# k and q of batch 0 loaded in two halves each, transposed in four groups, with the a1 copies on two engines around v's permute

## The chip, the cores and the metric

One core of a Trainium2 chip runs the kernel. The metric is the device time of one execution in microseconds (us). Most executions of one kernel agree within 0.3%. The profile's span is about 1.7 us shorter than the time (248.2 for 249.9). A run is called slow when it is over 1.5% above the fastest of its kernel.

## The reference, cut to what matters

```python
def sm_attn(qq, kk, vv):                   # q, k, v: 8 batches, 8 heads, 576 rows, 64
    s = scale * np.matmul(qq, kk.transpose(0, 1, 3, 2))
    a = softmax(s)                         # cut: max, exp, sum
    return np.matmul(a, vv)
p_packed = sm_attn(p, k, v)                # p: 32 rows per head
out = sm_attn(q, p_packed, p_packed)
# heads are joined to x (4608 x 512), then:
h = x @ w_in                               # 512 x 2048
return (h * np.cos(h)) @ w_out             # 2048 x 512
```

## The kernel before

The kernel works batch by batch. k and q have to be transposed by the matmul engine (PE), copied out of PSUM, where PE puts its results, by VectorE (DVE) or ScalarE (ACT), and multiplied. All large loads are issued from GpSimd (POOL) and convert float32 to bfloat16 on the way. In the listing, `s1` is the first softmax and a1 its exponentials, `pp` is a1 times v, `ppw` multiplies pp by a block of w_in (the result is PPW), and `s2` is the second softmax, with q. The opening, cut:

```python
def load(n, b):
    bf[n, b] = bf_pool.tile([TP, H, C * D], BF16, ...)       # 96 x 8 x 384
    G.dma_start(out=bf[n, b], in_=srcs[n][b].rearrange("h (p c) d -> p h (c d)", c=C))

def pe_T(n, b, engs, groups=(0, 1, 2), own=False):
    for i in groups:                                          # 3 groups of 8 transposes
        ...
        copy(engs[i], t[:, 8*i:8*i+8]..., ps[:, 0:8*TP])

nc.sync.dma_start(out=p_raw[:, 0:2, :], in_=p_rows[:, 0:2, :])
load("k", 0)
load("v", 0)
make_identity(nc, ident)
load("q", 0)
load("k", 1)
for n in range(3):
    load_w_in(n)
...                                       # constants
warm(7)                                   # matmuls on zeros, meant to keep PE's clock up
dup_p(0, 2, V); pack_p(0, 1)
warm(9)
pe_T("k", 0, (V, ACT, V))
ACT.dma_start(out=p_raw[:, 2:4, :], in_=p_rows[:, 2:4, :])
s1(0)                                     # first softmax: scores and exp
permute_v(0, V)
load("v", 1); load_w_in(3)
warm(3)
a1_pe(0)                                  # transposes of a1, copies by V
warm(2)
recips(0)
pp(0)                                     # a1 times v
pe_T("q", 0, (V, ACT, V))
load("q", 1)
for n in range(4):
    load_w_out(n)
G.dma_start(out=p_raw[:, 4:, :], in_=p_rows[:, 4:, :])
...
for fc in range(NFC):                     # h of batch 0, 16 steps
    rest = h_mm(0, fc)
    if fc in (11, 12, 13):
        pe_T("q", 1, (V, ACT, V), (fc - 11,), own=True)
    ...                                   # ppw at 1, 5, 8; pp(1) at 10; set_filler(0) at 13
    if fc >= 14:
        fill(2)                           # fill(n): n output matmuls (they need w_out)
...
fill(14)
slot(1, ...)                              # h of batch 1
```

The softmax here doesn't subtract the row's maximum and nothing guards it: scores larger than these inputs give would overflow.

Of the kernel before, what the change touches and what calls it, by code (L numbers as in the profile page):

```python
# [15 lines left out]
def kernel(  # L16
# [11 lines left out]
    B, H, S, D = q.shape  # L28
# [4 lines left out]
    C = 6  # L33
    TP = S // C
# [20 lines left out]
    V, ACT, G = nc.vector, nc.scalar, nc.gpsimd  # L55
# [13 lines left out]
    srcs = {"k": k, "q": q, "v": v}  # L69
    bf, vp, xT, a1T, sums1, r1, rs1 = {}, {}, {}, {}, {}, {}, {}  # L70
    a2u, lns, a2n, PPW = {}, {}, {}, {}

    def copy(eng, out, in_):
        if eng is ACT:
            ACT.copy(out=out, in_=in_)  # L75
        else:
            eng.tensor_copy(out=out, in_=in_)  # L77

    def psa(dt=FP32):
        return A.tile([128, 2, 512 if dt == FP32 else 1024], dt, name="psA", tag="A")  # L80

    def load(n, b):
        bf[n, b] = bf_pool.tile([TP, H, C * D], BF16, name=n + "bf", tag=n + "bf", bufs=2 if n == "k" else 1)
        G.dma_start(out=bf[n, b], in_=srcs[n][b].rearrange("h (p c) d -> p h (c d)", c=C))

    def permute_v(b, eng=G):
        vp[b] = vp_pool.tile([TP, C, H * D], BF16, name="vp", tag="vp")
        copy(eng, vp[b].rearrange("p c (h d) -> p c h d", h=H),
             bf["v", b].rearrange("p h (c d) -> p c h d", c=C))
# [2 lines left out]
        t = xT[n, b] = att_pool.tile([128, H * 3, TP], BF16, name=n + "T", tag=n + "T", bufs=2 if n == "k" else 1)  # L92
        nc.sync.dma_start_transpose(out=t, in_=bf[n, b].rearrange("p h x -> p (h x)"))

    def pe_T(n, b, engs=(V, V, V), groups=(0, 1, 2), own=False):
        if 0 in groups:
            xT[n, b] = att_pool.tile([128, H * 3, TP], BF16, name=n + "T", tag=n + "T", bufs=2 if n == "k" else 1)
        t = xT[n, b]
        flat = bf[n, b].rearrange("p h x -> p (h x)")
        for i in groups:  # L100
            ps = bank(BF16) if own else psa(BF16)[:, 0, :]
            for j in range(8):
                o = 8 * i + j
                nc.tensor.transpose(ps[:, j * TP:(j + 1) * TP], flat[:, o * 128:(o + 1) * 128],  # L104
                                    ident[0:TP, 0:TP])
            copy(engs[i], t[:, 8 * i:8 * i + 8].rearrange("p a x -> p (a x)"),
                 ps[:, 0:8 * TP])

    def bank(dt=FP32):
        return O.tile([128, 512 if dt == FP32 else 1024], dt, name="ot", tag="ot")  # L110

    def pack_p(b0, b1, flat=None):
        ng = 2 * (b1 - b0)
        if flat is None:
            flat = psa(BF16).rearrange("p a x -> p (a x)")
        for g in range(ng):
            nc.tensor.transpose(flat[:, g * 128:(g + 1) * 128],
                                p_bf[:, 2 * b0 + g].rearrange("p t d -> p (t d)"), ident)
        V.tensor_copy(out=P2[:, b0:b1].rearrange("p b h n -> p (b h n)"), in_=flat[:, 0:ng * 128])
# [14 lines left out]
    def s1(b, later=False):  # L134
        ps = scores(P2[:, b], xT["k", b])
        sm = sums1[b] = small.tile([128, 2], FP32, name="sums1")

        def exps():
            for y in range(2):
                ACT.activation(  # L140
                    out=a1[b % 2][:, y, :, 0:TP].rearrange("p (e m) x -> p e m x", e=2),
                    in_=ps[y][:, :, 0:HS].rearrange("p e (m x) -> p e m x", m=3),
                    func=AF.Exp, scale=scale, accum_out=sm[:, y:y + 1])
        if later:
            return exps
        exps()

    def recips(b):
        r1[b] = small.tile([128, 2], FP32, name="r1")
        rs1[b] = small.tile([128, 2], FP32, name="rs1")  # L150
        V.reciprocal(r1[b], sums1[b])
        V.tensor_scalar(out=rs1[b], in0=r1[b], scalar1=scale, scalar2=None, op0=ALU.mult)
# [3 lines left out]
        nc.sync.dma_start_transpose(out=t.rearrange("p a c x -> p (a c) x"),  # L156
                                    in_=a1[b % 2].rearrange("p a c x -> p (a c x)"))

    def a1_pe(b, ys=(0, 1), own=False):
        if 0 in ys:  # L160
            a1T[b] = att_pool.tile([128, 2, C, 128], BF16, name="a1T", tag="a1T")
        t = a1T[b]
        for y in ys:
            ps = bank(BF16) if own else psa(BF16)[:, 0, :]
            for c in range(C):
                nc.tensor.transpose(ps[0:TP, c * 128:(c + 1) * 128], a1[b % 2][:, y, c, 0:TP], ident)
            copy(V, t[0:TP, y].rearrange("p c x -> p (c x)"), ps[0:TP, 0:C * 128])

    def a1_one(b):
        t = a1T[b] = att_pool.tile([128, 2, C, 128], BF16, name="a1T", tag="a1T")  # L170
# [7 lines left out]
    def pp(b, own=False, engs=(V, ACT)):  # L178
        ps = bank() if own else psa()[:, 0, :]
        for hp in range(4):  # L180
            for j in range(C):
                c = 2 * (j % 3) + j // 3
                nc.tensor.matmul(ps[:, hp * 64:(hp + 1) * 64], vp[b][:, c, hp * 128:(hp + 1) * 128],  # L183
                                 a1T[b][0:TP, :, j, 32 * hp:32 * hp + 32], start=(j == 0), stop=(j == C - 1))
        pv = ps[:, 0:256].rearrange("p (a y x) -> p a y x", a=4, y=2)
        t = ppT[b % 2].rearrange("p (a y) x -> p a y x", y=2)
        for y in range(2):
            r = slice(64 * y, 64 * y + 64)
            copy(engs[0], t[r, :, y, :], pv[r, :, y, :])
        for y in range(2):  # L190
            r = slice(64 * y, 64 * y + 64)
            z = slice(64 - 64 * y, 128 - 64 * y)
            copy(engs[1], t[z, :, y, :], pv[r, :, y, :])
# [150 lines left out]
    def warm(n):  # L344
        wps = bank()
        for _ in range(n):
            nc.tensor.matmul(wps, wz[:, 0:128], wz, start=True, stop=True)  # L347

    nc.sync.dma_start(out=p_raw[:, 0:2, :], in_=p_rows[:, 0:2, :])
    load("k", 0)  # L350
    load("v", 0)
    make_identity(nc, ident)
    load("q", 0)
    load("k", 1)
    for n in range(3):
        load_w_in(n)
# [9 lines left out]
    warm(7)  # L366
    dup_p(0, 2, V)
    pack_p(0, 1)
    warm(9)
    pe_T("k", 0, (V, ACT, V))  # L370
    ACT.dma_start(out=p_raw[:, 2:4, :], in_=p_rows[:, 2:4, :])
    s1(0)
    permute_v(0, V)
    load("v", 1)
    load_w_in(3)
    warm(3)
    a1_pe(0)
    warm(2)
    recips(0)
    pp(0)  # L380
    pe_T("q", 0, (V, ACT, V))
    load("q", 1)
    for n in range(4):
        load_w_out(n)
# [5 lines left out]
    sums2(0, 0)  # L390
    sums2(0, 1)
    pe_T("k", 1, (V, V, V))
    warm(2)
    s1_mm = s1(1, later=True)
# [75 lines left out]
    s1(2)  # L470
    fill(5)
    a1_pe(2, (0,))
    fill(2)
    a1_pe(2, (1,))
    recips(2)
    fill(4)
# [94 lines left out]
```

## Time and profile before

| | before |
|---|---|
| median of the time, 6 runs | 249.91 us (249.81 to 250.28) |
| span of the profiled run | 248.2 us |
| PE, DVE, ACT busy | 234.5, 168.0, 166.9 us |
| first exponential of the first softmax (L140) | 9.78 us |
| first exponential of the second softmax (L225) | 16.05 us |
| k, q of batch 1 landed | 18.10, 33.43 us |
| last block of w_out landed | 43.70 us |

A landing is the moment at which the last of the 16 DMA engines has reported its share of a load; such times are from the trace's completion records.

### The profile page before, as it was taken

What the parts mean: (1) busy time and instruction counts of PE and PEld (TensorE: products, weight loads), DVE (VectorE), ACT (ScalarE), POOL (GpSimd) and SP (SyncE); (2) the same over time, 40 slices, a digit from 0 to 9 for tenths busy, and PEclk for the clock granted to TensorE, in tenths of its full rate; (3) what the DMA queues carried; (4) which work ended last, traced back from release to release, by engine and by line L of the source; (5) the groups of instructions that cost most, each with busy time, mean ns of one, the idle gap of its engine ahead of it and who ended that gap; (6) DMA issues with size and microseconds to landing.
All of it is one profiled execution on the core that took longest, in us unless ns stands there. A gap on an engine that the chain in (4) does not pass through costs nothing.

```text
span 248.2 us, 5035 instructions
## 1 busy us (share of the span) xinstructions
PE 234.5 (94%) x2003; PEld 131.6 (53%) x2037; DVE 168.0 (68%) x254; ACT 166.9 (67%) x278; POOL 54.8 (22%) x68
## 2 busy tenths in 40 slices
PE   8878799999999899999999999999999999999993
PEld 3454374566544654475546554565456554665452
DVE  2549987789568967678857766678766774876110
ACT  2368799746566787888877777888787684873000
POOL 8333533240400044022313105030500000000000
PEclk9999999999999999999999999999999999999999
DMA  6999999999899999999989995989491113201133
GB/s 91 203 203 206 205 206 229 200 241 153 162 206 219 167 158 220 206 193 173 190 162 192 174 194 68 177 164 209 103 156 33 45 42 82 47 26 58 46 83 85
DMA packets 63175, 37.09 MB, mean 149 GB/s; under 512 B 35792, under 2 KB 58576, under 8 KB 63152
## 3 DMA queue, kind: packets, MB, share of 16 engines
q0 software_dynamic: 23152, 18.75, 49.5%
q1 hardware_dynamic: 39568, 17.83, 34.3%
q8 instruction: 16, 0.26, 0.4%
q10 hardware_dynamic: 432, 0.20, 0.4%
q14 instruction: 7, 0.06, 0.1%
HBM read 37.22 MB, written 9.44 MB: 188 GB/s over the span
## 4 chain that ended last, share of the span: by engine, by line
PE 75%; DMA 9%; DVE 7%; ACT 5%; issue 2%; SPq 0%; DVEq 0%; ACTq 0%
PE ot L309 42%; PE psA L256 19%; DMA qbf<-in_q_dram 7%; DVE gT L263 4%; PE psA L207 3%; PE ot L347 3%; PE psA L183 2%; ACT cosT L260 2%; DMA out_dram<-osb 2%; PE psA L129 2%; PE ot L295 1%; PE psA L233 1%; DVE PPW L77 1%; ACT ppT L75 1%; PE psA L104 1%
## 5 line engine op out<-in xcount | busy, mean ns | idle before, releaser
L309 PE MATMUL ot<-w_out_bf,gT 128*128 128x512 bf16 x482 | 127.4, 379 | 2.1 <-issue 1.3
L263 DVE TENSOR_TENSOR gT<-psA,cosT 128x576 bf16<-128x576 f32 x128 | 93.6, 755 | 26.5 <-ACT cosT L260 25.9
L260 ACT ACTIVATE cosT<-psA 128x576 bf16<-128x576 f32 x128 | 82.5, 652 | 28.0 <-PE psA L256 23.2
L256 PE MATMUL psA<-a2n,PPW 128*128 128x288 bf16 x512 | 83.8, 286 | 1.9 <-DVE PPW L77 0.4
L309 PEld LDWEIGHTS <-gT 128*128 128x128 bf16 x512 | 47.7, 98 | 43.2 <-issue 6.7
L256 PEld LDWEIGHTS <-PPW 128*128 128x128 bf16 x512 | 49.3, 98 | 35.2 <-issue 4.4
L77 DVE CAST PPW<-psA 128x1024 bf16<-128x1024 f32 (+1 forms) x23 | 26.9, 1176 | 11.6 <-PE psA L207 11.5
L267 POOL COPY joint<-gT 128x512 bf16<-128x512 bf16 x16 | 9.8, 614 | 88.5 <-DVE gT L263 88.5
L77 DVE COPY osb<-ot 128x512 f32<-128x512 f32 (+1 forms) x24 | 16.3, 679 | 17.5 <-PE ot L309 7.6
L75 ACT COPY osb<-ot 128x512 f32<-128x512 f32 (+1 forms) x13 | 7.3, 565 | 15.3 <-PE ot L309 10.6
L77 POOL COPY vp<-vbf 96x3072 bf16<-96x3072 bf16 x6 | 16.5, 2751 | 3.8 <-DMA vbf<-in_v_dram 3.8
L243 DVE SCALAR_TENSOR_TENSOR a2n<-a2u,r,lns 128x576 bf16<-128x576 bf16 x16 | 12.3, 814 | 7.3 <-ACT lns L241 7.3
L140 ACT ACTIVATE a<-psA 128x576 bf16<-128x576 f32 x16 | 10.3, 647 | 7.1 <-PE psA L129 7.1
L235 ACT ACTIVATE lns<-psA 128x576 f32<-128x576 f32 x16 | 10.2, 650 | 7.1 <-PE psA L233 6.5
L309 PE MATMUL ot<-w_out_bf,joint 128*128 128x512 bf16 x46 | 12.4, 379 | 0.1
L225 ACT ACTIVATE a2u<-psA,rs 128x576 bf16<-128x576 f32 x16 | 11.0, 737 | 1.4 <-PE psA L129 1.3
L75 ACT CAST ppT<-psA 64x128 bf16<-64x128 f32 x24 | 6.2, 260 | 7.2 <-DVE ppT L77 5.9
L207 PE MATMUL psA<-w_in_bf,ppT 64*32 64x512 bf16 x224 | 10.2, 381 | 0.0
L347 PE MATMUL ot<-wz 128*128 128x512 bf16 x23 | 8.7, 524 | 1.4 <-DVE wz L358 1.2
L241 ACT ACTIVATE lns<-lns 128x576 f32<-128x576 f32 x16 | 10.0, 676 | 0.0
L183 PEld LDWEIGHTS <-vp 96*128 96x128 bf16 x192 | 6.6, 98 | 2.2 <-issue 1.1
L77 DVE COPY kT<-psA 128x768 bf16<-128x768 bf16 x8 | 4.2, 552 | 5.2 <-PE psA L104 5.1
(72 smaller groups left out, 150.8 us busy)
## 6 DMA issues: line engine op xcount, KB each, us to landing
kbf<-in_k_dram POOLq DMA_DIRECT2D x8, 576.0 KB, 12.0
vbf<-in_v_dram POOLq DMA_DIRECT2D x8, 576.0 KB, 7.3
qbf<-in_q_dram POOLq DMA_DIRECT2D x8, 576.0 KB, 9.6
out_dram<-osb SPq DMA_DIRECT2D x24, 192.0 KB, 2.6
out_dram<-osb SPq DMA_DIRECT2D x22, 128.0 KB, 2.4
w_in_bf<-in_moe_w_in_dram POOLq DMA_DIRECT2D x4, 512.0 KB, 17.5
w_out_bf<-in_moe_w_out_dram POOLq DMA_DIRECT2D x4, 512.0 KB, 20.4
out_dram<-osb SPq DMA_DIRECT2D x26, 64.0 KB, 2.1
```

What stands on the lines that cost most here:

```text
L75: ACT.copy(out=out, in_=in_)
L77: eng.tensor_copy(out=out, in_=in_)
L140: ACT.activation(out=a1[b % 2][:, y, :, 0:TP].rearrange("p (e m) x -> p e m x", e=2), in_=ps[y][:, :, 0:HS].rearrange("p e (m x) -> p e m ...
L183: nc.tensor.matmul(ps[:, hp * 64:(hp + 1) * 64], vp[b][:, c, hp * 128:(hp + 1) * 128], a1T[b][0:TP, :, j, 32 * hp:32 * hp + 32], start=(j ...
L207: nc.tensor.matmul(ps[y][32 * x:32 * x + 32, :], ppT[b % 2][r, 2 * x + y, :], w_in_bf[r, x, n * 512:(n + 1) * 512], start=True, stop=True)
L225: ACT.activation(out=a2u[b][:, y].rearrange("p (e x) -> p e x", e=2), in_=ps[y][:, :, 0:HS], func=AF.Exp, scale=rs1[b][:, y:y + 1])
L243: V.scalar_tensor_tensor(out=a2n[b][:, y], in0=a2u[b][:, y], scalar=r1[b][:, y:y + 1], in1=lns[b][:, y], op0=ALU.mult, op1=ALU.mult)
L256: nc.tensor.matmul(ps[:, e, 0:HS], PPW[b][:, y, fc * 128:(fc + 1) * 128], a2n[b][:, y, e * HS:(e + 1) * HS], start=(y == 0), stop=(y == 1))
L260: ACT.activation(out=csv, in_=ps[:, :, 0:HS], func=AF.Sin, bias=PI_HALF)
L263: V.tensor_tensor(out=gT[b][:, fc, :].rearrange("p (e x) -> p e x", e=2), in0=ps[:, :, 0:HS], in1=csv, op=ALU.mult)
L309: nc.tensor.matmul(pss[c], w, w_out_bf[:, fc, :], start=(fc == 0), stop=(fc == NFC - 1))
L347: nc.tensor.matmul(wps, wz[:, 0:128], wz, start=True, stop=True)
```

## The change

The intent is a shorter opening: the transposes of k begin when half of k is there, and likewise q; smaller copies finish sooner; the second a1 copy goes to ACT while DVE permutes v.

```diff
-    def load(n, b):
+    def load(n, b, parts=1):
+        for i in range(parts):
+            r = slice(i * H // parts, (i + 1) * H // parts)
+            G.dma_start(out=bf[n, b][:, r], in_=src[:, r])
 ...                     # pe_T: m transposes per group; a1_pe: eng for the copy
-    load("k", 0)
+    load("k", 0, 2)
     load("v", 0)
     make_identity(nc, ident)
-    load("q", 0)
+    load("q", 0, 2)
 ...
-    warm(9)
-    pe_T("k", 0, (V, ACT, V))
+    warm(6)
+    pe_T("k", 0, (V, ACT, ACT, V), (0, 1), m=6)
+    warm(2)
+    pe_T("k", 0, (V, ACT, ACT, V), (2, 3), m=6)
     s1(0)
-    permute_v(0, V)
     load("v", 1)
 ...
-    a1_pe(0)
+    a1_pe(0, (0,))
+    permute_v(0, V)
+    a1_pe(0, (1,), eng=ACT)
     warm(2)
     recips(0)
+    pe_T("q", 0, (V, ACT, V, V), (0, 1), m=6)
     pp(0)
-    pe_T("q", 0, (V, ACT, V))
+    pe_T("q", 0, (V, ACT, V, V), (2, 3), m=6)
```

More of the change, by code (lines that the diff above doesn't have):

```diff
@@ L80, in psa @@
         return A.tile([128, 2, 512 if dt == FP32 else 1024], dt, name="psA", tag="A")
-    def load(n, b):
+    def load(n, b, parts=1):
         bf[n, b] = bf_pool.tile([TP, H, C * D], BF16, name=n + "bf", tag=n + "bf", bufs=2 if n == "k" else 1)
-        G.dma_start(out=bf[n, b], in_=srcs[n][b].rearrange("h (p c) d -> p h (c d)", c=C))
+        src = srcs[n][b].rearrange("h (p c) d -> p h (c d)", c=C)
+        for i in range(parts):
+            r = slice(i * H // parts, (i + 1) * H // parts)
+            G.dma_start(out=bf[n, b][:, r], in_=src[:, r])
     def permute_v(b, eng=G):
@@ L93, in xbar, with pe_T @@
         nc.sync.dma_start_transpose(out=t, in_=bf[n, b].rearrange("p h x -> p (h x)"))
-    def pe_T(n, b, engs=(V, V, V), groups=(0, 1, 2), own=False):
+    def pe_T(n, b, engs=(V, V, V), groups=(0, 1, 2), own=False, m=8):
         if 0 in groups:
@@ L101, in pe_T @@
             ps = bank(BF16) if own else psa(BF16)[:, 0, :]
-            for j in range(8):
-                o = 8 * i + j
+            for j in range(m):
+                o = m * i + j
                 nc.tensor.transpose(ps[:, j * TP:(j + 1) * TP], flat[:, o * 128:(o + 1) * 128],
                                     ident[0:TP, 0:TP])
-            copy(engs[i], t[:, 8 * i:8 * i + 8].rearrange("p a x -> p (a x)"),
-                 ps[:, 0:8 * TP])
+            copy(engs[i], t[:, m * i:m * i + m].rearrange("p a x -> p (a x)"),
+                 ps[:, 0:m * TP])
     def bank(dt=FP32):
@@ L157, in a1_xbar, with a1_pe @@
                                     in_=a1[b % 2].rearrange("p a c x -> p (a c x)"))
-    def a1_pe(b, ys=(0, 1), own=False):
+    def a1_pe(b, ys=(0, 1), own=False, eng=V):
         if 0 in ys:
@@ L166, in a1_pe @@
                 nc.tensor.transpose(ps[0:TP, c * 128:(c + 1) * 128], a1[b % 2][:, y, c, 0:TP], ident)
-            copy(V, t[0:TP, y].rearrange("p c x -> p (c x)"), ps[0:TP, 0:C * 128])
+            copy(eng, t[0:TP, y].rearrange("p c x -> p (c x)"), ps[0:TP, 0:C * 128])
     def a1_one(b):
```

## The prediction

> **What bounds the kernel now.** The page first: time by engine, the slices, and the chain that ended last.
>
> ```profile
> PE 234.5 (94%) x2003; PEld 131.6 (53%) x2037; DVE 168.0 (68%) x254; ACT 166.9 (67%) x278; POOL 54.8 (22%) x68
> DMA  6999999999899999999989995989491113201133
> ...
> PE 75%; DMA 9%; DVE 7%; ACT 5%; issue 2%; SPq 0%; DVEq 0%; ACTq 0%
> ```
>
> PE is busy nearly everywhere, but in the opening part of that is filler: the line of warming matmuls on zeros. The DMA engines are full through the first half. The chain has one long DMA piece, so I asked for the chain in order of time, first 50 us. Its opening jumps over everything in between:
>
> ```profile
> 8.50 0.81 ACT kT L75
> 9.30 0.04 issue
> 9.35 0.41 PE psA L129 x6
> ...
> 14.57 0.51 PE psA L104 x8
> 15.09 0.28 issue
> 15.37 18.06 DMA qbf<-in_q_dram
> 33.43 0.05 issue
> 33.48 0.51 PE ot L104 x8
> ```
>
> The load of q of batch 1 is issued at 15.37 us, when the transposes of q of batch 0 have freed its buffer, and lands 18.06 us later, at 33.43. PE's transposes start 0.05 us after that, and from there the chain is compute. The chain view ties the landing to its issue; whether an earlier issue would mean an earlier landing is the whole question. The DMA view of the first 50 us answers it:
>
> ```profile
> DMA  0259999999999999999999999999999999999999
> GB/s 0 52 35 170 201 201 205 200 205 201 195 205 215 200 203 207 206 207 203 205 213 199 206 202 204 209 205 204 208 204 208 218 197 281 238 192 198 205 203 203
> ```
>
> Each slice is 1.25 us. From about 4 us on, the engines are saturated at some 200 GB/s (of the narrow type written). The trace's packet records show one first-in first-out stream: k0 moved from 2.9 us, v0 from 6.7, q0 from 9.6, k1 from 12.6, three blocks of w_in from 15.8, v1 from 23.5, w_in's last from 26.4, q1 from 29.0. So q1 waited in the queue for 13.6 of its 18.06 us. It lands after a fixed number of bytes: 6 loads of 0.59 MB and 4 of 0.52 MB, 5.64 MB, which at 0.203 MB per us is 27.8 us; with the start at 2.9 us, 0.9 us lost in k0 (3.8 us where v0 took 2.9) and 1.5 us from the first engine's completion to the last one's, that makes 33.1, near the measured 33.43.
>
> The timeline shows that the work between is in step with the same stream:
>
> ```profile
> 13.36 0.75 PEld L104 LDWEIGHTS <-qbf 96*128 96x128 bf16 x17 [0.24 <-DMA qbf<-in_q_dram]
> ...
> 18.15 1.19 PE L104 MATMUL psA<-ident,kbf 96*128 96x96 bf16 x24 [0.27 <-DMA kbf<-in_k_dram]
> ...
> 30.55 0.41 PE L207 MATMUL ot<-w_in_bf,ppT 64*32 64x512 bf16 x8 [0.60 <-DMA w_in_bf<-in_moe_w_in_dram]
> ```
>
> PE waits for q0 at 13.3, for k1 at 18.1, for w_in's last block at 30.5 and for q1 at 33.4. Completion records give the landings (last of 16 engines): k0 7.27, v0 10.18, q0 13.32, k1 18.10, w_in 19.98, 22.55, 25.07, v1 28.12, w_in 30.51, q1 33.43. Each is a gate where a lead gained before is lost.
>
> **What the Trainium skill says.** "DMA: Bandwidth & Descriptors", section "Issuing engines are not separate DMA queues": all DMAs run on the same 16 engines and interleave, whoever starts them, and issuing time is usually small beside the transfer. The trace agrees: an issue costs POOL 0.77 us for 2.9 us of transfer. The same page, section "Anatomy of one DMA": a fixed cost of about 2 us per DMA that is mostly completion latency, not setup. Queued back to back it is hidden here: v0's first packet follows k0's last at 6.7 us with no hole. The section on why a DMA increments its semaphore by 16: only the full 16 means landed. The trace agrees, and it matters: k1's engines finished from 15.91 to 18.10. "Runtime: NRT & Kernel Launch", section "Instruction fetch mechanics": instructions come by DMA in blocks of 16 KiB. The trace has 16 such records in a queue of their own, one at 16.05 us taking 0.94 us, which is where k1's spread comes from (first to last engine 0.69 us for q0, 2.19 for k1, then about 1.5 for every later load).
>
> **The change part by part.**
> Halves of k0. Half of k0 is 0.29 MB. 384 of its rows had started by about 5.2 us; with 0.5 us for completion the first half lands near 5.7, the second near 7.3 as now. PE gets there after the first warming and packing (4.57) and six instead of nine warming matmuls (0.36 each, 2.2 us): 6.7. Twelve transposes at 0.043 are 0.5, two warming matmuls about 0.6, twelve transposes 0.5: last transpose at about 8.4 where it was 8.8 (7.62 + 1.19). Copies are 576 wide instead of 768: by their ratio 0.44 us on DVE (0.56 to 0.62 now) and 0.61 on ACT (0.80). Last copy ends near 9.0 instead of 9.4, the scores follow: gain about 0.4 us.
> a1 around the permute. Now DVE does permute 0.96 and then two copies of 0.6, 10.20 to 12.34. New: first a1 copy about 10.7 to 11.3, permute to 12.3, second copy on ACT (about 0.8) from 11.4 to 12.2. pp starts at about 12.3 instead of 12.39: no gain beyond 0.1, the k lead is spent on v's permute. v1 is issued some 0.9 us later, about 12.3, which is free: its bytes move at 23.5.
> q in halves. The first half of q0 lands near 11.9, and its transposes go ahead of pp. The second half still lands at 13.3. pp's own copies on DVE end near 13.9, then two copies of 0.44 to 14.8, scores then, first exponential at about 15.2 instead of 16.05. Gain about 0.8 us there.
> Then k1. Its transposes wait until 18.1 as before; DVE takes its three kT copies at 18.70 and, in order behind them, the normalisation at 20.10 and PPW's copies at 21.56, which let the first h matmul go at 22.37. The 0.8 us lead turns into a longer wait for k1. Even if k1 let something through, w_in's last block at 30.5 and q1 at 33.4 take it.
> Issue costs. Two more DMAs on POOL, near 0.7 us each (768 rows cost 0.77, 512 rows 0.75), delay the later issues by 1.4 us, far from harm: w_in's first block was issued at 4.99 and moved at 15.75. POOL's waits for finished loads, eight back, shift together with the two that are added, so later loads wait for the same ones. In the stream the two extra completions cost about 0.02 us each. A shorter first issue may start the stream about 0.1 us sooner (first packet now 0.69 us after the issue ended).
> Sum: q1's landing -0.1 us, everything after it is unchanged code. 249.9 - 0.1 = 249.8 us.
>
> **Rivals.**
> (a) The lead of 0.8 us goes through to the end: 249.1. For it: the chain names the opening's PE, ACT and DVE pieces up to 15.1. Against it: the queue is never empty, and q1 is 13.6 us back in it at its issue.
> (b) The whole stream moves with its start. If descriptors of half a load are out in half the time, the first packet comes 0.4 us sooner and q1 with it: 249.5. Against: issue time hardly depends on rows. If splitting costs the stream something, the other way: 250.2.
> (c) The instruction fetches fall elsewhere, since PE is ahead and two instructions shorter. k1's last engine could then finish sooner or later by up to 1 us; but the engine that carries the fetch still has it to do before q1, so it shows at k1 and hardly at q1. If two fetches gather on one engine, q1 is late by up to 0.9 us: 250.7.
> (d) PE idles longer before k1 with fewer warming matmuls and its clock falls. The page shows the granted clock at full in all slices, and the new idle time is under 1 us, so I give it little.
>
> **Range and chances.** The stream's start and spread are worth -0.4 to +0.3, and runs of before spread by 0.13. I choose 249.2 to 250.3 around 249.8. Two per cent is 5 us, far outside each rival: faster 0.01, same 0.98, slower 0.01.
>
> **What would show it.** k0's copies should end near 9.0 and the first exponential of the second softmax (L225 now) begin near 15.2; then PE's wait for k1 should grow from 0.3 to about 1 us, with k1 landing near 18.1; the wait for w_in at 30.5 and q1's landing within 0.4 us of 33.4. A landing of q1 well before 33, or transposes of q1 that start well after it, would prove the prediction wrong; so would a hole in the stream, or a first h matmul much later than 22.4.

## The result, and the profile after

The changed kernel took 250.54 us in the median of 6 runs (250.03 to 250.87), the kernel before 249.91. The ratio is 1.0021, with a 95% interval of 1.0009 to 1.0034. A ratio here is the mean time of one kernel's fast runs over that of the other's in the same rounds, so it is not quite the ratio of the medians. The change made the kernel slower by about 0.5 us. The profiled run was a fast one.

The table view by stretches of time shows the first place where the two part. Columns: stretch, its length, busy us (and instructions) of PE, PE's weight loads, DVE, ACT and POOL, PE's granted clock, the DMA engines' share, and GB/s. The kernel before:

```profile
2.00:6.00 4.00, 4.00 (x12) 1.57 (x11) 0.94 (x5) 0.02 (x1) 3.92 (x8) 1.00 0.91 125
6.00:10.00 4.00, 3.58 (x46) 2.13 (x46) 1.11 (x2) 1.02 (x2) 1.26 (x2) 1.00 1.31 202
10.00:14.00 4.00, 3.54 (x55) 2.43 (x55) 2.95 (x8) 1.17 (x5) 1.54 (x2) 1.00 1.31 200
```

The changed kernel:

```profile
2.00:6.00 4.00, 4.00 (x12) 1.57 (x11) 0.91 (x5) 0.02 (x1) 3.92 (x8) 1.00 0.97 139
6.00:10.00 4.00, 3.55 (x48) 1.91 (x46) 0.92 (x2) 1.78 (x3) 2.42 (x4) 1.00 1.19 148
10.00:14.00 4.00, 2.68 (x41) 1.75 (x40) 2.18 (x5) 1.83 (x6) 1.21 (x2) 1.00 1.30 198
```

The last column decides. The stream starts a little better (139 for 125), then runs at 148 GB/s from 6 to 10 us where it ran at 202, and is normal again afterwards. In the packet records of those 4 us, 592 KB were moved where it had been 808, the mean packet of 768 bytes took 98 ns instead of 79, and 58 of 771 packets took over 100 ns, where 2 of 1052 had. By 10 us the stream was 165 KB behind (1099 for 1264). At 200 KB per us that is 0.8 us, and the queue did not make it up: q of batch 1 landed 0.69 us later and w_out's last block 0.76. The engines' busy share fell too, from 1.31 to 1.19, so the packets did not only take longer, there were also fewer under way at a time.

The work that waits for loads further back in the queue is later by nearly as much, 0.6 to 0.8 us. From the timeline of the changed kernel:

```profile
9.50 0.65 ACT L143 ACTIVATE a<-psA 128x576 bf16<-128x576 f32 x1 [0.46 <-PE psA L132]
...
13.11 0.69 PE L107 MATMUL psA<-ident,qbf 96*128 96x96 bf16 x12 [1.22 <-DMA qbf<-in_q_dram]
...
16.58 1.37 ACT L228 ACTIVATE a2u<-psA,rs 128x576 bf16<-128x576 f32 x2 [0.82 <-PE psA L132]
...
18.79 1.20 PE L107 MATMUL psA<-ident,kbf 96*128 96x96 bf16 x24 [0.38 <-DMA kbf<-in_k_dram]
...
31.26 0.41 PE L210 MATMUL ot<-w_in_bf,ppT 64*32 64x512 bf16 x8 [0.65 <-DMA w_in_bf<-in_moe_w_in_dram]
...
34.16 0.52 PE L107 MATMUL ot<-ident,qbf 96*128 96x96 bf16 x8 [0.22 <-DMA qbf<-in_q_dram]
```

The two exponentials in the kernel before:

```profile
9.78 0.65 ACT L140 ACTIVATE a<-psA 128x576 bf16<-128x576 f32 x1 [0.49 <-PE psA L129]
...
16.05 1.37 ACT L225 ACTIVATE a2u<-psA,rs 128x576 bf16<-128x576 f32 x2 [0.71 <-PE psA L129]
```

The first exponential does come earlier, 9.50 for 9.78. Then PE stands 1.22 us before the first half of q, and the second softmax begins at 16.58 where it had begun at 16.05. k of batch 1 is taken up at 18.79 instead of 18.15, and q of batch 1 at 34.16 instead of 33.48.

The chain of waits in order of time has changed its DMA link, from q of batch 1 to w_in's second block and, issued by POOL once that had landed, w_out's last. The changed kernel:

```profile
6.92 16.31 DMA w_in_bf<-in_moe_w_in_dram
23.23 0.28 issue
23.51 20.95 DMA w_out_bf<-in_moe_w_out_dram
44.46 0.04 issue
44.51 0.81 PE ot L312 x3
```

PE's output matmuls go on 0.04 us after w_out's last block has landed, at 44.46. In the kernel before, that block landed at 43.70 and PE's record for the same three matmuls (in the view from 44 us on) begins at 43.74:

```profile
43.74 0.81 PE L309 MATMUL ot<-w_out_bf,gT 128*128 128x512 bf16 x3
```

So there was a second gate behind q1 which the chain view had not named. In the instruction records the output matmuls ahead of it start 0.22 us apart, and the one that needed the block started 0.38 us after its neighbour in the kernel before and 0.44 us in the changed one. PE thus lost only 0.16 and 0.22 us there: it reaches this gate just ahead of the block, and by this an earlier block alone would have gained no more than that. Span minus that landing is 204.50 us in both profiles (248.2 - 43.70; 249.0 - 44.46, each with one more digit than printed here).

### The profile page after: what moved, and what is told of

Read it like the earlier page. It is cut to its first block, busy times and chain, and to the rows that moved or that the text cites. A ratio compares the mean times of both kernels' runs of the same rounds, so it can differ in the third digit from the quotient of the medians.

```text
span 249.0 us, 5072 instructions
## 1 busy us (share of the span) xinstructions
PE 236.5 (95%) x2036; PEld 131.1 (53%) x2036; DVE 167.9 (67%) x254; ACT 167.9 (67%) x280; POOL 55.9 (22%) x70
## 3 DMA queue, kind: packets, MB, share of 16 engines
q0 software_dynamic: 23184, 18.75, 49.5%
## 4 chain that ended last, share of the span: by engine, by line
PE 71%; DMA 15%; DVE 6%; ACT 3%; POOL 2%; issue 1%; DVEq 0%; POOLq 0%
PE ot L312 43%; PE psA L259 19%; DMA w_out_bf<-in_moe_w_out_dram 8%; DMA w_in_bf<-in_moe_w_in_dram 7%; DVE gT L266 4%; PE psA L210 3%; ACT cosT L263 2%; PE psA L186 2%; PE psA L132 2%; PE ot L298 1%; PE psA L236 1%; DVE PPW L77 1%; POOL kbf L87 1%; ACT ppT L75 1%; DVE a2n L246 1%
## 5 line engine op out<-in xcount | busy, mean ns | idle before, releaser
L312 PE MATMUL ot<-w_out_bf,gT 128*128 128x512 bf16 x512 | 133.3, 380 | 0.1
L246 DVE SCALAR_TENSOR_TENSOR a2n<-a2u,r,lns 128x576 bf16<-128x576 bf16 x16 | 12.3, 813 | 7.3 <-ACT lns L244 7.3
L87 POOL DMA_DIRECT2D vbf<-in_v_dram x8 | 6.2, 776 | 6.4 <-DVE rs L155 4.4
L77 DVE COPY kT<-psA 128x768 bf16<-128x768 bf16 (+1 forms) x8 | 4.0, 526 | 5.2 <-PE psA L107 5.2
```

What stands on the lines that cost most here:

```text
L77: eng.tensor_copy(out=out, in_=in_)
L246: V.scalar_tensor_tensor(out=a2n[b][:, y], in0=a2u[b][:, y], scalar=r1[b][:, y:y + 1], in1=lns[b][:, y], op0=ALU.mult, op1=ALU.mult)
L312: nc.tensor.matmul(pss[c], w, w_out_bf[:, fc, :], start=(fc == 0), stop=(fc == NFC - 1))
```

## The experiments

Theories after the result. **A**: splitting the loads slows the queue. **B**: the new order of the compute does. **C**: the trace caught a chance stall. Eighteen runs were made, e1 of the changed kernel again and the others of variants. All gave the right result; g1's side load is not used by it. This table holds what the arguments use: the median, the ratio to the kernel before of the same rounds with its interval, the KB that the load queue moved from 6 to 10 us, the landing of w_out's last block, and span minus that landing. "Slow run" and "PE idle" mark profiles with a lowered PE clock or a stall behind the gate, to which the last column does not apply; in e2 and f4 the clock fell too, but from 15.5 and 16.1 us for 3.4 us, ahead of the gate, where it cost nothing. A landing is from one profile: in the five kernels whose loads are all whole and in their old order (before, e4, g4, h1, h2) w_out's last block landed from 43.67 to 44.27 us, so a smaller difference between two landings says little by itself. g1 and g2 are single runs, whose state is unknown.

| run | median us | ratio (95%) | KB 6-10 us | w_out | rest |
|---|---|---|---|---|---|
| before | 249.91 | | 808 | 43.70 | 204.5 |
| changed | 250.54 | 1.0021 (1.0009, 1.0034) | 592 | 44.46 | 204.5 |
| e1_again | 250.64 | 1.0025 (1.0012, 1.0038) | 659 | 44.85 | slow run |
| e2_k_dma | 250.69 | 1.0026 (1.0014, 1.0038) | 635 | 44.64 | 204.5 |
| e3_q_dma | 249.84 | 1.0001 (0.9989, 1.0013) | 811 | 43.86 | 204.5 |
| e4_whole | 250.00 | 1.0004 (0.9991, 1.0016) | 807 | 44.08 | slow run |
| f1_v_dma | 250.00 | 0.9999 (0.9982, 1.0016) | 803 | 43.83 | 204.5 |
| f2_k_rows | 250.41 | 1.0021 (1.0003, 1.0040) | 770 | 43.88 | 204.5 |
| f3_k_q_v | 255.13 | 1.0202 (1.0187, 1.0218) | 673 | 43.83 | (PE idle) |
| f4_k_id_v | 251.42 | 1.0046 (1.0026, 1.0067) | 608 | 45.02 | 204.5 |
| f5_p_first | 250.42 | 1.0018 (1.0003, 1.0033) | 810 | 44.29 | 204.6 |
| g1_lag | 255.55 | one run | 700 | 44.66 | (PE idle) |
| g2_v_first | 254.10 | one run | 803 | 43.37 | (PE idle) |
| g3_k_6_2 | 249.94 | 1.0006 (0.9987, 1.0024) | 759 | 43.76 | 204.5 |
| g4_q1_later | 250.27 | 1.0007 (0.9993, 1.0021) | 805 | 44.11 | 204.6 |
| h1_fill11 | 250.80 | 1.0032 (1.0020, 1.0045) | 807 | 43.67 | 205.3 |
| h2_later_fill13 | 250.22 | 1.0011 (0.9998, 1.0023) | 809 | 44.27 | 204.6 |
| h3_p_ahead | 251.18 | 1.0049 (1.0035, 1.0062) | 806 | 44.78 | 204.5 |
| i1_p_early | 250.00 | 1.0004 (0.9991, 1.0017) | 794 | 43.91 | 204.5 |
| i2_order_p_early | 252.45 | 1.0053 (1.0011, 1.0096) | 795 | 44.35 | slow run |

### Which part of the change costs the time

**e1_again**: the changed kernel, unedited.

> The changed kernel once more, unedited, for a second trace. In its first trace the queue of loads moved only some 130 to 165 KB per us from 6 to 10 us where the kernel before moved 200, and q of batch 1 landed at 34.12 instead of 33.43. Theory A (splitting the loads slows the queue each time): again a slow stretch, q1 at 33.9 or later, 250.5. Theory C (a chance stall that one trace caught): no slow stretch, q1 near 33.4, and a time near 249.9.

**e2_k_dma**: the kernel before and only this.

```diff
-    load("k", 0)
+    load("k", 0, 2)
```

> The kernel before with only k of batch 0 loaded as two halves; no compute instruction differs. Theory A with k as the culprit: a slow stretch after k0, q1 at about 34.1, 250.5. If q's split is the culprit: 249.8 to 250.0. Theory B (the order of the compute, not the loads): 249.9.

**e3_q_dma**: the same for q alone.

```diff
-    load("q", 0)
+    load("q", 0, 2)
```

> The kernel before with only q of batch 0 loaded as two halves. Theory A with q as the culprit: q1 at about 34.1, 250.5. If k's split is the culprit: 249.9. Theory B: 249.9.

**e4_whole**: the changed kernel with both loads whole, its order of the compute kept.

```diff
-    load("k", 0, 2)
+    load("k", 0)
-    load("q", 0, 2)
+    load("q", 0)
```

> The changed kernel with its two loads whole again (one DMA each), all its changed compute order kept. Theory A: the stream is that of the kernel before, q1 at 33.4, 249.9. Theory B: 250.5 with q1 late although nothing is split.

The slow stretch came again in e1 and, with not one compute instruction changed, in e2, whose time is that of the whole change (ratio 1.0026 for 1.0021). Its stretch from 6 to 10 us, with e3's after it:

```profile
6.00:10.00 4.00, 3.52 (x50) 2.08 (x49) 1.11 (x2) 1.78 (x4) 1.86 (x3) 1.00 1.19 159
```

```profile
6.00:10.00 4.00, 2.84 (x45) 1.73 (x45) 1.12 (x2) 1.06 (x2) 1.86 (x3) 1.00 1.31 203
```

e3 and e4 run at the full rate and take the time of the kernel before. So the loss is k's split, not q's (A, for k alone); the new order in itself neither gains nor loses in fast runs (B falls), by the times of e4, whose trace is a slow run's; and it is not chance (C falls).

### What it is about k's halves

**f1_v_dma**: v in two halves, second in the queue, k whole.

```diff
-    load("v", 0)
+    load("v", 0, 2)
```

> The kernel before with only v of batch 0 (second in the queue) in two halves, k whole. All three kernels with k in halves had a slow stretch of the load queue from 6 to 10 us (about 160 KB per us for 200), none with k whole had, q in halves or not. Theory 1 (what counts is that the queue's first load is short, so that the next ones are queued while the engines already run): no slow stretch, 1.25 to 1.27 MB moved by 10 us, 249.9. Theory 2 (any split ahead of a load slows it, q's only hidden by its place): a slow stretch, under 1.2 MB by 10 us, 250.5.

**f2_k_rows**: k in two halves by partitions instead of heads.

```diff
-            r = slice(i * H // parts, (i + 1) * H // parts)
-            G.dma_start(out=bf[n, b][:, r], in_=src[:, r])
+            r = slice(i * TP // parts, (i + 1) * TP // parts)
+            G.dma_start(out=bf[n, b][r], in_=src[r])
```

> The kernel before with k of batch 0 in two halves by rows of partitions (0 to 47, 48 to 95, all heads) instead of by heads. Theory 1 (a short first load): slow stretch as with heads, under 1.2 MB by 10 us, 250.5. Theory 3 (the addresses: four heads of each row, then the other four, set the engines against each other): no slow stretch, 1.26 MB by 10 us, 249.9 or a little less.

**f3_k_q_v**: k in halves, then q ahead of v.

```diff
     load("k", 0, 2)
-    load("v", 0)
+    load("q", 0)
     make_identity(nc, ident)
-    load("q", 0)
+    load("v", 0)
```

> k of batch 0 in halves by heads, and the queue's order of v and q of batch 0 exchanged. The slow stretch of the other runs fell on v's load. If v's addresses are what is slow after halves of k: 6 to 10 us is quick now and the slow stretch comes with v from about 9.5 us. If it is the place in the queue or the time: q is slow from 6 to 10 us, under 1.2 MB by 10 us. The time of the whole is not compared here, since v comes later for pp: 250.5 to 251.5.

**f4_k_id_v**: k in halves, then the identity, then v.

```diff
     load("k", 0, 2)
-    load("v", 0)
     make_identity(nc, ident)
+    load("v", 0)
     load("q", 0)
```

> k of batch 0 in halves by heads, nothing else changed but that the identity is built between them and v's load, so that v is queued some 0.6 us later, still 2 us before its bytes move. If v's being queued while the first half starts is what makes the stream slow: 200 KB per us from 6 to 10 us and 249.6 to 250.0. If not: a slow stretch as before, 250.5.

**f5_p_first**: k whole behind a small load.

```diff
+    G.dma_start(out=p_raw[:, 2:4, :], in_=p_rows[:, 2:4, :])
     load("k", 0)
 ...
-    ACT.dma_start(out=p_raw[:, 2:4, :], in_=p_rows[:, 2:4, :])
```

> The kernel before with k whole, but with the small load of p (64 KB) moved from ACT's queue to the front of the same queue, so that k is the second load and is queued while the engines already run. Theory 1 (a short first load): a slow stretch follows within some us and q1 lands late, 250.3 to 250.6. Theory 3 (k's halves and their addresses): none; the stream is later by p's 64 KB at most, 0.2 to 0.3 us, which the ACT load cost in the middle anyway: 249.9.

**g1_lag**: eight of the sixteen engines kept busy longer behind k.

```diff
     load("k", 0)
+    G.dma_start(out=side, in_=moe_w_in[0:32].rearrange("(a p) n -> p a n", p=8))
     load("v", 0)
```

> The kernel before, k whole, with a side load of 8 partitions put between k and v of batch 0, which keeps 8 of the 16 engines busy about 1.3 us longer (4 rows of 4 KB each at some 13 KB per us), so that the engines go on out of step. The result is unused. Theory 4 (engines that are out of step slow each other, which is what halves of k brought about): packets over 100 ns again and under 170 KB per us in the stretch behind the side load. Theory 1 or 3 (something of the short first load by heads): all packets near 79 ns, 200 KB per us. The whole time is 0.7 to 1.5 us over before in either case, by the extra bytes.

**g2_v_first**: v whole, then k in halves.

```diff
-    load("k", 0, 2)
     load("v", 0)
+    load("k", 0, 2)
```

> The queue begins with v of batch 0, whole, and k of batch 0 in halves by heads comes second. Theory 5 (halves by heads slow only as the first of the queue, whose start is ragged): 200 KB per us from 5 us on. If k's halves slow wherever they stand: a slow stretch from about 9 us. The whole time is worse than before by 2 us or more, since k comes 2.9 us later; only the stream is compared.

**g3_k_6_2**: k as six heads and two.

```diff
-        for i in range(parts):
-            r = slice(i * H // parts, (i + 1) * H // parts)
+        for r in ((slice(0, 6), slice(6, 8)) if parts == 2 else (slice(0, 8),)):
```

> The kernel before with k of batch 0 as six heads and two heads instead of four and four. If raggedness left by a short first load is the cause, a longer first load gives less of it: over 1.2 MB by 10 us and about 250.1. If any division by heads of the first load brings the slow stretch: under 1.2 MB by 10 us and 250.5.

The slow stretch is reproducible: all five kernels that begin their queue with halves of k by heads (the changed one, e1, e2, f3, f4) moved 592 to 673 KB from 6 to 10 us, and every kernel that begins with a whole load, or with p, moved 794 to 811, apart from g1 with its side load. What the cause is not:

- Not any load in halves: v's halves (f1) and q's (e3) run clean, and so do k's own halves when v goes first. g2's row reads 201 GB/s:

```profile
6.00:10.00 4.00, 1.48 (x16) 0.72 (x14) 0.56 (x1) 0.00 (x0) 1.85 (x3) 1.00 1.31 201
```

- Not the short first load alone: behind p (f5) the stream starts late and raggedly, 352 KB by 6 us for 456, and then runs at the full rate. f5 loses its time at the start, so that its 250.42 lies in theory 1's range by chance.
- Not v's addresses: with q in v's place (f3) q was the slow one. f3's median of 255.13 says nothing about the stream: PE waited for v from 11 to 16 us and its clock fell to half from 15.0 to 25.2 us.
- Not that v is queued as early as it is: the identity in between (f4) did not help. Leaving f3 aside, f4 is even the slowest of the five, with w_out's last block at 45.02; why is not known.

The shape of the parts may matter, but this is not settled. In their traces rows (f2, 770 KB) and six heads with two (g3, 759 KB) slow the stretch much less than four and four do, and g3's time is close to that of the kernel before (1.0006). But f2's ratio is 1.0021, as large as that of the change. f2's profiled run was one of its two quick ones, at 250.17, and its two others took 250.64 and 251.14, so its trace does not stand for all of its runs. g1 was to show whether engines out of step slow one another, and it is inconclusive: behind the side load packets were slow as theory 4 had expected, from 8.0 to 9.5 us (mean 159, 211 and 113 ns in the three halves of a us), but from 9.5 us on they took 79 to 81 ns on average, although v's share still landed 1.5 us apart on the first and the last engine. Why the packets behind k's halves take longer stays open; no run here shows what they wait for.

### What sets the end

**g4_q1_later**: loads as before, PE given other work while q1 is on its way.

```diff
-        if fc in (11, 12, 13):
-            pe_T("q", 1, (V, ACT, V), (fc - 11,), own=True)
+        if fc in (12, 13, 14):
+            pe_T("q", 1, (V, ACT, V), (fc - 12,), own=True)
 ...                     # ppw's third at 9, pp(1) at 11, set_filler at 14, fill from 15
```

> The kernel before with loads unchanged, but the transposes of q of batch 1 one step of the h loop later, and with them the last block of PPW, pp of batch 1 and the first output chunks, so that PE has work while q1 is on its way. If q1's landing at 33.4 is what sets the end (my theory of where the time is decided): PE waits less for w_in's last block and for q1, 249.2 to 249.7. If PE's own work sets it: 249.9 as before, or a little more from the moved filler.

PE did come earlier, and then stood at the next gate:

```profile
44.15 0.38 PE L309 MATMUL ot<-w_out_bf,gT 128*128 128x512 bf16 x1 [0.43 <-DMA w_out_bf<-in_moe_w_out_dram]
```

The expectation of 249.2 to 249.7 missed, at 250.27. In its profile the block landed at 44.11, 0.4 us later than in the profile of before, and the span followed. The ratio, 1.0007 (0.9993 to 1.0021), is not clear of noise.

**h3_p_ahead**: that block alone delayed, by putting p's rest ahead of it.

```diff
-    for n in range(4):
+    for n in range(3):
         load_w_out(n)
     G.dma_start(out=p_raw[:, 4:, :], in_=p_rows[:, 4:, :])
+    load_w_out(3)
```

> The kernel before with the load of p's rest (384 KB as written) put ahead of w_out's last block in the queue; q1 and all before it keep their places. If w_out's last block sets the end: it lands 1.5 to 2 us later (p took 1.4 us of the stream), and the span is its landing plus 204.5 us, so 251.3 to 251.9. If q1's landing at 33.4 sets the end, as I predicted: 249.9 to 250.2.

q1 landed at 33.57, nearly as before, and the block at 44.78, 1.08 us later. The profiled span rose by 1.1 us. PE's wait:

```profile
44.82 0.81 PE L309 MATMUL ot<-w_out_bf,gT 128*128 128x512 bf16 x3 [0.95 <-DMA w_out_bf<-in_moe_w_out_dram]
```

The time, 251.18, is under the range expected because the block was delayed less than I had worked out, 1.08 instead of 1.5 to 2 us; the rule of 204.5 us held.

**h1_fill11** and **h2_later_fill13**: only so many output matmuls ahead of the next h loop as can do without that block; h1 on the kernel before, h2 on g4.

```diff
-    fill(14)
+    fill(11)        # h2: fill(13)
     slot(1, ...
```

> The kernel before with 11 instead of 14 output matmuls ahead of the h loop of batch 1, so that just the 24 that need only the first three blocks of w_out stand before it. If w_out's last block sets the end: PE goes on with h while it lands, span minus that landing falls below 204.5, 249.4 to 249.8. If not: 249.9 to 250.1.

> The earlier run with q1's transposes later, in which PE came 0.4 us early to w_out's last block and waited for it, with 13 instead of 14 output matmuls ahead of the h loop (24 in all that need three blocks). If that block was what stopped it: 249.3 to 249.7. If something else stops it: 250.2 as there.

Both missed. In h1 PE passed the gate without a wait, but the same output matmuls then had to be done later. In its timeline PE waits for DVE's copy of an output tile, which it did not in the kernel before:

```profile
48.29 0.38 PE L309 MATMUL ot<-w_out_bf,gT 128*128 128x512 bf16 x1 [0.56 <-DVE osb L77]
```

h2's profile shows the same: PE goes on with h at 43.68, ahead of the block's landing at 44.27, and then has the same wait of 0.56 us at 48.23.

So in h3 the gate cost one for one when the block came later, and in h1 and h2 it gave nothing back when PE was only led around it.

**i1_p_early** and **i2_order_p_early**: p's second 64 KB moved from the midst of the stream to before it; i1 on the kernel before, i2 on the changed kernel with k whole.

```diff
     nc.sync.dma_start(out=p_raw[:, 0:2, :], in_=p_rows[:, 0:2, :])
+    nc.sync.dma_start(out=p_raw[:, 2:4, :], in_=p_rows[:, 2:4, :])
 ...
-    ACT.dma_start(out=p_raw[:, 2:4, :], in_=p_rows[:, 2:4, :])
```

> The kernel before with p's second 64 KB loaded at the very start behind the first 64 KB, instead of at 8.5 us by ACT. In the kernel before some 80 KB less than usual pass between 12 and 13.5 us, 0.4 us of stream. If the stream sets the end: w_out's last block lands near 43.3 instead of 43.7, the span follows, 249.5. If the early p delays the stream's start by as much: 249.9.

> The changed kernel with k of batch 0 whole, q in halves, all its changed order, and p's second 64 KB early as in the other run. If the stream alone decides, the changed order gives nothing: w_out's last block near 43.3 and 249.5, as the other run, in the runs without a lowered clock. If the order helps: 0.2 us or more below the other.

i1 gained nothing, and its trace tells why. The dip at 12 to 13.5 us is gone, and the first engine had w_out's last block at 41.80 instead of 42.11. But a last share was behind from the start: k landed from 6.94 to 8.23 us over the 16 engines, where it had been 6.82 to 7.27. From there to w_out's last block, at 43.91, the last share comes about 0.5 us behind the one before it; that it is one engine each time is likely, but the records do not name the engine. A landing is that of the slowest engine. i2 is inconclusive: only two of its six runs were undisturbed, at 249.86 and 250.08, again the time of the kernel before. No kernel here beat the kernel before.

### The slow runs

Of 11 timed runs of the changed kernel one was slow (255.21, in e1), of the other variants e2 had one of 6, e4 two of 7, f4 one of 4, i2 two of 6; none of 53 runs of the kernel before was above 250.53. e1's profile fell into one, and shows what happened there. The clock row of its page (a digit for each 6 us, in tenths) has two dips:

```profile
PEclk9959979999999999999999999999999999999999
```

After the first, PE was behind. Then a small instruction of DVE met POOL's permute of v. e1:

```profile
28.98 3.25 DVE L155 TENSOR_SCALAR rs<-r 128x2 f32<-128x2 f32 x1
29.43 2.75 POOL L77 COPY vp<-vbf 96x3072 bf16<-96x3072 bf16 x1
```

The changed kernel in its fast profile:

```profile
28.04 0.17 DVE L155 TENSOR_SCALAR rs<-r 128x2 f32<-128x2 f32 x1
29.75 2.75 POOL L77 COPY vp<-vbf 96x3072 bf16<-96x3072 bf16 x1
```

An instruction of 0.17 us took 3.25 us and ended with POOL's copy, at 32.2. PE then waited 3.09 us for DVE. The same stands in the slow profiles of e4 (3.45 us) and i2 (3.02 us), where it also ended with the copy. "SBUF — State Buffer" of the Trainium skill, section "Who interferes with whom", says that DVE and GpSimd share a pair of ports under an exclusive lock; the trace agrees with that in how the stall ends. It does not show how the stall begins: in all three DVE's instruction started 0.2 to 0.7 us ahead of the copy, while POOL was still issuing k's load. In the fast profiles of the kernel before and of the changed one, the two pass 1.6 and 1.5 us apart. Whether the shorter warming of the changed order lets the clock fall more often was not tested by itself: e2 and f4, which keep the old warming and have k in halves, had a slow run each too, and the clock fell once even in their fast profiles.

## Why the prediction was wrong

- **What bounds the opening** was right: one full queue, and a lead in the compute that is lost at the next landing. e4's times show it: the changed order with whole loads takes 250.00 in the median, the time of the kernel before.
- **Halves of k.** The first half landed at 5.73, as predicted (5.7), the second at 7.88 instead of 7.3. PE waited 0.21 us for it, and the gain at the first exponential was 0.28 us instead of 0.4.
- **a1 around the permute.** pp was to start at 12.3 and started at 13.63. PE's order has q's first transposes ahead of it, and the first half of q came at 13.06 instead of 11.9. In e3, where the stream is not slowed, that half landed at 11.83, so it was the slow stream that made it late. The wait of 1.22 us there is a new one, which the change put in pp's way.
- **q in halves.** The second softmax was to gain 0.8 us and lost 0.53 (16.58 for 16.05).
- **k1 and the gates.** k1 was to land near 18.1 and landed at 18.75; PE's wait for it was to grow to about 1 us and was 0.38.
- **The step that failed** is the cost of the issues in the stream: "In the stream the two extra completions cost about 0.02 us each", and with it "q1's landing -0.1 us". In place of -0.1 us, q1 landed 0.69 us later and w_out's last block 0.76 us, in this pair of profiles; the times rose by about 0.5 us. It was not the completions, of which e3 and f1 have one more each at no loss: k's halves made the packets behind them slower for 4 us. That is the "hole in the stream" which the prediction had named as a sign against itself; why packets slow down stays open. The start of the stream did come sooner, as I had allowed for (507 KB by 6 us for 456), and the slow stretch took that back and more. Rival (b) had "If splitting costs the stream something, the other way: 250.2"; it was the right one, with too small a size, and the range's upper end of 250.3 was built on it.
- **The gate that I named was one of two.** I had the end follow q1's landing. w_out's last block stands 0.04 us ahead of PE's matmuls in both profiles, and h3, which delays it alone, moves the end by the same 1.1 us. As both are in the same stream, it does not alter the sum.
- **The chances** were right: 0.98 for within 2%, and it was 0.2%.

## What to carry to other kernels

When a full load queue paces the work, ask of a change first what it does to the queue, and only then what it does to the compute. Splitting the first load of a queue need not be free even if its issue is hidden; run the split alone, without the compute that is to profit, and compare the bytes moved in each stretch. Here a stall at 6 to 10 us still stood at the end of the queue in the changed kernel (0.76 us), though not in all variants: in f3, where more was shifted, the queue was 78 KB behind at 10 us and the last block only 0.13 us late. A load has landed when its slowest engine is done, and behind the gate that a chain names there may stand the next one.

## What the Trainium skill lacked or had wrong

- "DMA: Bandwidth & Descriptors": nothing in it says that cutting the first load of a queue can slow the loads behind it. Here k's halves by heads gave 592 to 673 KB in the 4 us behind them, in five kernels, where 794 to 811 are usual.
- The same page, section "Anatomy of one DMA", gives a fixed cost of about 2 us for each DMA. In a queue that never empties it does not show: v's last completion packet began at 9.86 us and v had landed at 10.18, and one DMA more cost nothing where it was not the first (e3, f1: ratios 1.0001 and 0.9999).
- "Runtime: NRT & Kernel Launch", section "Instruction fetch mechanics", calls the cost of a block mostly hidden. It is not hidden from a full load queue: the fetch at 16.05 us took 0.94 us, and the spread between first and last engine, 0.69 us for q0, was 2.19 for k1 and 1.5 to 1.7 for the loads behind it. In e4, where the fetch came at 17.20, k1 still landed within 0.69 us and the spread of 1.6 began with the next load.
- "TensorE: Matmul & The Clock Gate", Part 1, has the clock fall after an idle window of about 3.4 us. In e1 it fell to half at 13.42 us, when PE's longest wait in the 9 us before it had been 1.43 us.
